# Retention and a two-layer MLP on one core: loads written as flat rows, the state cleared on GpSimd, and a new order of the early tasks

## The chip, the cores and the metric

The kernel runs on one core of one Trainium2 chip. The metric is the device time of one execution in microseconds (us); the kernel before was run three times, and its profile is that of one execution. The core has five engines, each with its own instruction stream that is worked through in order: PE (TensorE, matmuls and transposes), DVE (VectorE), ACT (ScalarE), POOL (GpSimd) and SP (SyncE). Transfers between device memory and on-chip memory are issued by an instruction on POOL, ACT or SP and are then carried out by 16 DMA engines that all issuers share. PEld in the profile is the loading of matmul weights, which overlaps PE.

## What is computed

```
B, H, S, D = 4, 8, 768, 64           # q, k, v: [B, H, S, D] float32
for t in range(S):
    state = gamma[h] * state + outer(k[t], v[t])        # per batch and head, D x D
    y[t]  = q[t] @ state / sqrt(D)
x  = y as [B, S, H*D]                                   # 4 x 768 x 512
xn = (x - mean(x)) / sqrt(var(x) + 1e-6) * g_ln
out = x + relu(xn @ w_ch1) @ w_ch2                      # 512 -> 2048 -> 512, float32
```

## The kernel before

The recurrence is worked in chunks of 128 positions. Six chunks in each of four batches make 24 tiles of 128 rows by 512 columns. Tiles 0 to 3 are the first chunk of each batch; tiles 4 to 8 are chunks 1 to 5 of batch 0; then come the other batches. For tile t, PE transposes k and q (lines 498 and 505, "tk" and "tq"; from tile 8 on a DMA transpose of the pair of both, line 520, does it), DVE scales q (line 510 or 527), PE multiplies k by q (line 538, "pa"), DVE applies the decay mask (line 562), and PE multiplies the result by v and adds the state's part (lines 582 and 586, or 548 and 572, "py"). DVE then takes mean and variance (lines 601 and 602) and subtracts the mean (line 613, "xn"); ACT keeps a copy of x (line 619); the centred tile is transposed (line 672, "tx", or a DMA transpose, line 686).

The state of a batch is carried on by four steps: POOL scales v by the decay (line 633, "vg"), PE multiplies it by k into `pd` (line 645), and DVE writes it, scaled, into one of two `state` tiles (line 659). Only the diagonal 64 by 64 blocks of a state tile are written there; the rest has to be zero, and is cleared once at the beginning (line 341).

The MLP takes tiles in groups: eight groups of one tile, four of two, two of four. The first layer ("m1", line 719) makes 2048 hidden values in steps of 512, each needing a quarter of `w_ch1` ("w1_0" to "w1_3"); ACT or DVE applies the relu (lines 732, 734). The second layer ("m2", line 757) sums over all hidden values, and its first matmul of a tile waits for all four quarters of `w_ch2` ("w2_0" to "w2_3"). DVE multiplies by the inverse deviation and adds x (line 767), and ACT issues the store (line 774).

**Loads.** All of q, k, v but k0 and q0, and the eight quarters of the weights, are loaded by DMAs that POOL issues, since they change float32 to bfloat16 (lines 430 and 438). One load of q, k or v is a tile of 128 rows, 8 heads, 64 values (128 KB written); one quarter of a weight is 512 KB written. The source of such a load has 64 values in a row, since heads lie far apart. From tile 8 on, each load on POOL stands behind a "gate" (line 447), a tiny copy that waits until an earlier load has landed. At most eight such loads are outstanding: POOL waits 0.56 us before the load at 16.76 until the one eight places earlier has landed at 16.48.

**The order of the work** is written out by hand. `plan.add` numbers the tasks in the order in which they are made. `ORDER` lists these numbers, and tasks are emitted in that order, so that it alone sets the sequence on each engine (100000 and 10000 added to a number choose a buffer or an engine). A planner with estimated durations (`load_pad` and `w_pad` are added to its landing times) computes start times from it; they set only how many filler matmuls (line 785) PE gets in early gaps, to keep it busy. The task numbers of POOL that matter here are:

```
v0 23  k1 24  q1 25  v1 26   k2 27  q2 28  v2 29   k3 30  q3 31  v3 32
k4 33  q4 34  v4 35  k5 36   q5 37  v5 38  k6 39   q6 40  v6 41  k7 42  q7 43  v7 44
w1_0..w1_3 45..48   w2_0..w2_3 49..52   k8 53  q8 54  v8 55
vg of v0, v4, v5, v6: 214 217 234 251     clearing of the state: 13 (zerod)
```

Of the kernel before, what the change touches and what calls it, by code (L numbers as in the profile page):

```python
# [14 lines left out]
PE, ACT, DVE, POOL, SP = range(5)  # L15
# [4 lines left out]
              "k3", "q3", "v3", "w1_2", "k4", "q4", "v4", "k5", "q5", "v5", "w1_3", "w2_0",  # L20
              "k6", "q6", "v6", "k7", "q7", "v7", "w2_1", "w2_2", "w2_3"],
    "bufs": {"qsb": 6, "ksb": 5, "vsb": 9, "qk": 8, "tr": 6, "vg": 3, "trq": 3, "trk": 3},
    "load_pad": 600, "w_pad": 550, "lead": 32, "lead2": 32, "sq_at": 28000, "late_load": 1700, "two": 4, "m2b": ("b0",), "m2all": 16, "inter": 4, "every": 4, "tail": (0, 384, 512), "step": 8, "pace": 8, "ahead": 3,
    "slack": 600, "tr_pad": 4000, "x_pad": 3500, "vg_pad": 2500, "fill": 0.8, "fill_end": 14000,
}

ORDER = [int(x) for x in """
16 17 2 0 3 19 20 23 14 8 15 1 24 5 7 9 25 4 10 6 13 21 11 26 18 45 22 27 44 28 146 46  # L30
100147 149 148 150 151 29 30 31 32 47 162 152 165 214 33 100163 153 164 154 155 166 156
12 167 158 157 159 168 34 176 160 35 36 100177 169 179 524 178 170 180 215 172 526 171
173 525 174 181 527 182 183 184 534 190 37 532 100191 38 10535 193 48 217 186 192 175
10533 194 49 185 187 540 195 536 39 541 234 40 196 197 537 204 207 544 198 100205 206
528 200 43 52 216 545 50 42 41 201 51 542 208 543 188 224 10529 199 218 209 100225 548
550 210 227 549 219 226 551 55 211 53 235 554 251 54 212 189 552 555 228 553 56 229 220
546 530 213 275 202 547 230 538 100241 221 10531 556 231 232 539 242 57 558 244 100237
557 233 222 238 560 161 243 10559 236 561 245 258 100259 562 246 260 566 247 563 261 564
567 252 262 570 248 249 223 254 565 255 568 60 250 569 203 263 268 100722 61 58 253 59
62 287 298 63 723 716 724 301 66 264 67 64 717 65 725 269 718 571 719 265 726 266 720  # L40
576 100271 270 276 307 267 578 272 579 577 728 273 68 69 278 277 72 729 730 731 318 73
279 70 299 71 280 580 572 732 281 300 282 74 322 284 286 734 735 75 288 239 581 283 285
736 302 303 290 289 573 737 291 738 574 319 584 292 740 741 293 320 294 296 742 308 304
240 585 78 575 743 582 744 295 297 310 333 79 76 309 77 339 586 305 583 311 80 746 587
334 747 312 335 313 314 274 316 323 81 256 315 748 84 350 749 351 588 592 317 325 85 82
83 379 750 589 257 324 354 326 727 602 86 752 87 753 327 328 329 603 593 590 754 755 594
591 330 90 331 340 352 332 342 756 341 343 721 380 598 321 599 595 91 758 336 759 344
760 761 596 733 88 345 89 355 762 346 368 348 353 600 92 757 745 739 337 597 347 93 764
96 349 97 94 381 601 95 765 98 338 357 604 356 766 606 386 99 605 382 607 767 358 306
359 383 614 612 768 360 384 615 361 613 363 770 397 102 771 103 100 362 772 398 365 364  # L50
763 369 101 104 371 370 773 403 610 372 608 774 611 373 776 616 609 399 366 105 374 387
108 109 617 375 618 414 367 377 106 107 777 620 418 751 376 378 389 619 110 388 778 390
779 622 415 391 385 404 780 392 393 621 623 630 782 395 111 114 429 115 631 394 112 400
456 113 433 626 116 624 117 396 406 120 121 416 405 430 783 627 625 407 784 431 408 628
419 409 634 785 410 629 632 411 412 457 118 119 122 413 421 635 786 445 633 420 123 788
126 458 422 127 789 646 124 423 424 790 425 427 647 401 125 426 428 791 642 638 434 436
792 435 794 795 796 639 643 465 769 437 438 640 417 439 440 442 128 797 459 641 129 441
446 443 476 132 644 798 432 402 133 645 636 130 448 447 648 131 134 138 637 460 650 449
450 649 800 651 461 451 452 801 802 477 454 803 444 775 480 462 453 466 478 455 135 491
804 136 137 468 492 467 806 139 495 807 469 470 140 493 808 471 141 809 472 142 474 473  # L60
475 652 653 654 481 483 482 484 810 655 656 658 143 510 479 485 144 787 506 805 657 799
145 659 660 661 486 662 507 496 487 489 664 663 488 508 490 666 498 497 665 499 667 668
670 669 500 671 501 502 672 673 504 511 812 674 503 505 676 513 512 675 514 678 463 677
680 515 679 682 813 681 814 683 516 494 811 509 517 781 519 464 518 520 815 100830 831
816 521 832 818 819 200824 820 825 684 817 793 685 826 690 688 691 827 689 694 696 833
695 522 686 697 687 708 709 821 698 699 692 693 523 822 848 700 828 834 702 100842 701
703 706 707 704 200836 714 837 705 715 712 838 849 843 713 710 711 850 844 845 839 846
851 840 100854 852 855 856 823 847 841 835 829 853 857 860 861 858 862 863 864 859 865
""".split()]


# [90 lines left out]
def kernel(  # L162
# [175 lines left out]

    def c_zero(eng):
        for x in state:  # L340
            nc.vector.memset(x, 0.0)

    a = plan.add
    small = a(DVE, 1200, -100, c_small)
# [11 lines left out]
    qscd = a(ACT, 700, -91, c_qsc, [args, table])  # L356
    maskd = a(DVE, 1230, -50, c_mask, [vscd, tri])
    gchd = a(ACT, 900, 100, c_gch, [small, qscd, vscd], at=9000)
    zerod = a(DVE, 480, -94, c_zero)
    exps = [gchd, qscd, vscd]  # L360

    def c_gb(eng):
# [17 lines left out]
    def load(kind, j, rank):  # L380
        takes, uses, follows = None, [], []
        if kind in "qkv":
            b, c = TILES[j]
            src = {"q": q, "k": k, "v": v}[kind][b].rearrange("h (c p) d -> c p h d", p=P)[c]
            ns, dma = 900, 875 if j < 9 else CFG["late_load"]
            pair = kind != "v" and j >= T0
            name = "qk" if pair else kind + ("0" if c == 0 and kind != "q" else "sb")
            takes = where[kind, j] = (name, j)
            if pair and kind == "q":
                takes, uses, follows = None, [takes], [loaded["k", j]]  # L390

            if j == 0 and kind in "kq":
                raws = []
                for half, eng in ((0, SP), (1, ACT)):
                    hs = slice(half * H // 2, (half + 1) * H // 2)

                    def emit32(eng, half=half, hs=hs):
                        if half == 0:
                            take("osb", kind, [P, DM], FP32)
                        dst = held["osb", kind].rearrange("p (h d) -> p h d", d=D)[:, hs]  # L400
                        (nc.scalar if eng == ACT else nc.sync).dma_start(out=dst, in_=src[:, hs])
                    raws.append(a(eng, 480, -200 + half + 2 * (kind == "q"), emit32, (),
                                  ("osb", kind) if half == 0 else None,
                                  [("osb", kind)] if half else [],
                                  lat=1200 if kind == "k" else 1700, follows=raws[:]))
                parts = []
                for half, eng in ((0, DVE), (1, ACT)):
                    if kind == "k":
                        half, eng = None, ACT

                    def emit(eng, half=half):
                        if not half:
                            take(*takes, [P, H, D], BF16)
                        hs = slice(0, H) if half is None else slice(4 * half, 4 * half + 4)
                        evacuate(eng, held[takes][:, hs],
                                 held["osb", kind].rearrange("p (h d) -> p h d", d=D)[:, hs])
                    parts.append(a(eng, 620 if half is None else 350, -60, emit,
                                   raws + parts[:1], takes if not half else None,
                                   [("osb", kind)] + ([takes] if half else [])))
                    parts[-1]["after"] = raws[:]  # L420
                    parts[-1]["follows"] = parts[:-1]
                    if kind == "k":
                        break
                loaded[kind, j] = parts
                return

            def emit(eng):
                if takes:
                    take(*takes, [P, 2, H, D] if pair else [P, H, D], BF16)
                nc.gpsimd.dma_start(out=tile_of(kind, j), in_=src)  # L430
        else:
            s = slice(j * DM, (j + 1) * DM)
            o = slice(j * KO, (j + 1) * KO)
            src, dst = (w1_v[:, :, s], w1[:, :, s]) if kind == "w1" else (w2_v[:, o, :], w2[:, o, :])
            ns, dma = 790, 2550

            def emit(eng):
                nc.gpsimd.dma_start(out=dst, in_=src)  # L438
# [382 lines left out]
```

## Time and profile before

| | |
|---|---|
| median of 3 runs | 220.67 us (220.42 to 221.4) |
| the profiled execution | 220.67 us, of which its span 218.9 us |
| busy in the span | PE 205.5 us, DVE 121.3, POOL 95.8, ACT 85.3 |
| software DMA queue (POOL's loads) | 77,024 packets, 13.37 MB, 79.8% of 16 engines' span |
| mean granted TensorE clock | 0.992 of full speed |
| PE waiting for a load of k | 3.2 us, once |

The span runs from the first to the last instruction of the program; the remaining 1.8 us of the execution lie around it. The chain of waits follows the work that ended last back to the beginning, and puts each stretch down to the engine or transfer that was being waited for. The table of stretches gives, for each part of the span, how long each engine was busy, the granted TensorE clock (PEclk, 1.00 is full speed) and what the DMA engines did.

### The profile page before, as it was taken

What the parts mean: (1) busy time and instruction counts of PE and PEld (TensorE: products, weight loads), DVE (VectorE), ACT (ScalarE), POOL (GpSimd) and SP (SyncE); (2) the same over time, 40 slices, a digit from 0 to 9 for tenths busy, and PEclk for the clock granted to TensorE, in tenths of its full rate; (3) what the DMA queues carried; (4) which work ended last, traced back from release to release, by engine and by line L of the source; (5) the groups of instructions that cost most, each with busy time, mean ns of one, the idle gap of its engine ahead of it and who ended that gap; (6) DMA issues with size and microseconds to landing.
All of it is one profiled execution on the core that took longest, in us unless ns stands there. A gap on an engine that the chain in (4) does not pass through costs nothing.

```text
span 218.9 us, 4937 instructions
## 1 busy us (share of the span) xinstructions
PE 205.5 (94%) x2005; PEld 131.9 (60%) x2027; DVE 121.3 (55%) x264; ACT 85.3 (39%) x173; POOL 95.8 (44%) x149
## 2 busy tenths in 40 slices
PE   6978999499999999999999999999999999999992
PEld 2457899396656676666766766675454444444451
DVE  6866686524547877655765686588786510030041
ACT  5476466434133242424424532352266611444200
POOL 8997398049877475573774656403000000000000
PEclk9999999969999999999999999999999999999999
DMA  9999999999999999999999999978541170000035
GB/s 128 176 179 179 162 187 165 191 118 106 109 106 116 97 124 141 169 189 206 114 151 209 87 153 127 118 108 117 101 161 27 28 215 3 0 0 0 0 141 197
DMA packets 108890, 26.85 MB, mean 123 GB/s; under 512 B 101569, under 2 KB 105921, under 8 KB 108866
## 3 DMA queue, kind: packets, MB, share of 16 engines
q0 software_dynamic: 77024, 13.37, 79.8%
q1 hardware_dynamic: 27186, 6.59, 20.8%
q10 hardware_dynamic: 4656, 6.56, 8.7%
q8 instruction: 16, 0.26, 0.5%
q14 instruction: 8, 0.07, 0.1%
HBM read 27.30 MB, written 6.29 MB: 153 GB/s over the span
## 4 chain that ended last, share of the span: by engine, by line
PE 78%; DMA 12%; POOL 7%; issue 1%; DVE 1%; DVEq 0%; POOLq 0%
PE b L757 35%; PE mm L719 33%; DMA ksb<-in_k_dram 5%; DMA w<-in_moe_w_ch_dram 5%; PE pa L538 2%; DMA out_dram<-osb 2%; POOL qsb L430 2%; PE pd L645 2%; PE b L572 2%; POOL v L430 2%; PE b L548 2%; POOL w L438 1%; POOL k L430 1%; DVE osb L767 1%; POOL vg L633 0%
## 5 line engine op out<-in xcount | busy, mean ns | idle before, releaser
L719 PE MATMUL mm<-xnt,w 128*128 128x128 bf16 (+2 forms) x896 | 96.8, 260 | 0.8 <-DMA w<-in_moe_w_ch_dram 0.8
L757 PE MATMUL b<-w,h 128*128 128x512 bf16 (+2 forms) x379 | 88.4, 370 | 1.2 <-issue 0.2
L732 ACT ACTIVATE h<-mm 128x512 bf16<-128x512 f32 x91 | 53.8, 598 | 87.0 <-PE mm L719 86.8
L719 PEld LDWEIGHTS <-w 128*128 128x128 bf16 x896 | 67.1, 99 | 21.5 <-DMA w<-in_moe_w_ch_dram 1.2
L757 PEld LDWEIGHTS <-h 128*128 128x128 bf16 x400 | 37.0, 98 | 37.7
L562 DVE TENSOR_TENSOR asb<-pa,mask 128x1024 bf16<-128x1024 f32 x24 | 29.3, 1222 | 19.1 <-PE pa L538 18.5
L767 DVE SCALAR_TENSOR_TENSOR osb<-b,rstd,x_all 128x512 f32<-128x512 f32 (+2 forms) x25 | 18.0, 726 | 26.9 <-PE b L757 26.6
L601 DVE BATCH_NORM_STATS2 bns<-b 128x6 f32<-128x256 f32 (+1 forms) x40 | 17.8, 477 | 22.3 <-PE b L586 11.2
L619 ACT CAST x_all<-b 128x256 bf16<-128x256 f32 (+1 forms) x40 | 16.2, 416 | 24.0 <-DVE xn L613 21.8
L633 POOL TENSOR_TENSOR vg<-vsb,vsc 128x512 bf16<-128x512 bf16 x16 | 16.6, 1041 | 19.3 <-DMA vsb<-in_v_dram 11.3
L613 DVE SCALAR_TENSOR_TENSOR xn<-b,mv,gb 128x256 bf16<-128x256 f32 (+1 forms) x40 | 20.1, 532 | 0.7
L430 POOL DMA_DIRECT2D vsb<-in_v_dram x20 | 18.2, 912 | 1.6 <-DMA qsb<-in_q_dram 0.8
L659 DVE TENSOR_TENSOR state<-pd,gch 64x256 bf16<-64x256 f32 x40 | 16.6, 415 | 3.7 <-PE pd L645 2.8
L430 POOL DMA_DIRECT2D qk<-in_q_dram x16 | 14.2, 890 | 1.7 <-issue 1.7
L430 POOL DMA_DIRECT2D qk<-in_k_dram x16 | 14.3, 891 | 1.5 <-issue 1.4
L447 POOL COPY scrap<-qk 1x1 bf16<-1x1 bf16 x30 | 5.5, 184 | 11.3 <-DMA qk<-in_q_dram 5.8
L447 POOL COPY scrap<-vsb 1x1 bf16<-1x1 bf16 x15 | 2.6, 176 | 15.0 <-DMA vsb<-in_v_dram 15.0
L700 DVE RECIPROCAL rstd<-rstd 128x1 f32<-128x1 f32 (+2 forms) x14 | 2.1, 156 | 12.2 <-ACT rstd L694 12.1
L785 PE MATMUL pd<-zeros 128*128 128x512 bf16 (+1 forms) x24 | 6.4, 405 | 1.3 <-DVE zeros L291 1.2
L572 PEld LDWEIGHTS <-asb 128*128 128x128 bf16 x128 | 5.8, 98 | 2.4
L527 DVE TENSOR_TENSOR trq<-tr,qsc 128x512 bf16<-128x512 bf16 x16 | 7.0, 439 | 0.1
L430 POOL DMA_DIRECT2D qsb<-in_q_dram x7 | 6.4, 915 | 0.0
(68 smaller groups left out, 128.1 us busy)
## 6 DMA issues: line engine op xcount, KB each, us to landing
out_dram<-osb ACTq DMA_DIRECT2D x23, 256.0 KB, 3.8
w<-in_moe_w_ch_dram POOLq DMA_DIRECT2D x8, 512.0 KB, 8.7
vsb<-in_v_dram POOLq DMA_DIRECT2D x20, 128.0 KB, 5.0
qk<-in_k_dram POOLq DMA_DIRECT2D x16, 128.0 KB, 4.9
qk<-in_q_dram POOLq DMA_DIRECT2D x16, 128.0 KB, 4.5
qsb<-in_q_dram POOLq DMA_DIRECT2D x7, 128.0 KB, 6.5
v<-in_v_dram POOLq DMA_DIRECT2D x4, 128.0 KB, 6.8
ksb<-in_k_dram POOLq DMA_DIRECT2D x4, 128.0 KB, 9.2
```

The source lines that it names most:

```text
L430: nc.gpsimd.dma_start(out=tile_of(kind, j), in_=src)
L562: nc.vector.tensor_tensor(out=take("asb", t, [P, NPAIR, 2, P], BF16).rearrange("p i a t -> p a i t"), in0=held["pa", t], in1=mask.rearrang ...
L572: nc.tensor.matmul(half_y[h % 2][:, h // 2 * D:(h // 2 + 1) * D], lhsT=held["asb", t][:, h // 2, h % 2, :], rhs=tile_of("v", t)[:, h, :], ...
L601: nc.vector.bn_stats(out=bns[:, t, i, :], in_=x)
L613: nc.vector.scalar_tensor_tensor(out=dst, in0=src, scalar=mv[:, t, 0:1], in1=g, op0=ALU.subtract, op1=ALU.mult)
L619: nc.scalar.copy(out=dst, in_=src)
L633: e.tensor_tensor(out=take("vg", j, [P, H, D], BF16), in0=tile_of("v", j), in1=vsc[:, cc, :].unsqueeze(2).to_broadcast([P, H, D]), op=ALU. ...
L659: nc.vector.tensor_tensor(out=held["pb", n][o, :, o], in0=held["pd", b][o, :, o], in1=gch[o, cc, :].unsqueeze(2).to_broadcast([D, NPAIR, D ...
L719: nc.tensor.matmul(p[:, j, :], lhsT=w1[:, ko, (ho + j) * P:(ho + j + 1) * P], rhs=held["xnt", hb][:, h0:h0 + n, ko, :], start=(ko == 0), s ...
L732: nc.scalar.activation(out=dst, in_=src, func=AF.Relu)
L757: nc.tensor.matmul(held[key][:, 0:w], lhsT=held["h1", hb][:, ho, i * P:(i + 1) * P], rhs=w2[:, ho, cols], start=(ho == 0), stop=(ho == HO ...
L767: nc.vector.scalar_tensor_tensor(out=take("osb", key, [P, w], FP32), in0=held[key][:, 0:w], scalar=rstd[:, t:t + 1], in1=x_all[:, t, cols] ...
```

## The change

There are four edits.

1. A load of q, k or v names its destination as a row of 512 values per partition in place of eight pieces of 64.
2. The two state tiles are cleared by POOL in place of DVE, at a later place in the order.
3. The planner's estimate of a weight's landing (`w_pad`) goes from 550 to 1500 ns.
4. `ORDER` is another one in its first 230 of 866 tasks; behind them only five small tasks of DVE (161, 175, 189, 223 and 239) stand elsewhere.

```diff
-    "load_pad": 600, "w_pad": 550, ...
+    "load_pad": 600, "w_pad": 1500, ...
 ORDER = [int(x) for x in """
-16 17 2 0 3 19 20 23 14 8 15 1 24 5 7 9 25 4 10 6 13 21 11 26 18 45 22 27 44 28 146 46
-100147 149 148 150 151 29 30 31 32 47 162 152 165 214 33 100163 153 164 154 155 166 156
-12 167 158 157 159 168 34 176 160 35 36 100177 169 179 524 178 170 180 215 172 526 171
-173 525 174 181 527 182 183 184 534 190 37 532 100191 38 10535 193 48 217 186 192 175
-10533 194 49 185 187 540 195 536 39 541 234 40 196 197 537 204 207 544 198 100205 206
-528 200 43 52 216 545 50 42 41 201 51 542 208 543 188 224 10529 199 218 209 100225 548
-550 210 227 549 219 226 551 55 211 53 235 554 251 54 212 189 552 555 228 553 56 229 220
+16 17 2 0 3 19 20 23 14 8 15 1 24 5 7 9 25 4 10 6 21 11 26 18 22 146 45 100147 149 148
+27 150 28 151 153 46 162 100163 29 152 154 164 165 30 155 12 166 31 156 167 32 157 158
+159 47 168 176 13 524 169 179 214 100177 170 525 33 215 178 171 172 216 180 34 173 181
+532 35 526 36 533 182 37 190 527 534 183 193 38 100191 184 535 48 192 185 186 194 187
+195 49 540 542 541 196 204 543 528 197 39 207 100205 198 536 529 40 200 42 43 41 206 544
+50 217 234 52 51 53 10537 55 208 100224 54 199 201 545 550 209 225 548 551 210 227 44
+226 251 202 549 552 228 218 56 211 546 553 547 222 275 212 219 538 229 235 220 100241
 ...
     def c_zero(eng):
         for x in state:
-            nc.vector.memset(x, 0.0)
+            nc.gpsimd.memset(x, 0.0)
 ...
-    zerod = a(DVE, 480, -94, c_zero)
+    zerod = a(POOL, 500, 0, c_zero, at=9000)
 ...
-                nc.gpsimd.dma_start(out=tile_of(kind, j), in_=src)
+                nc.gpsimd.dma_start(out=tile_of(kind, j).rearrange("p h d -> p (h d)"), in_=src)
```

On POOL the order of loads thus goes from the first to the second line of each pair; what stands before k2 is the same in both. Names in brackets are not loads.

```
before  k2 v7 q2 w1_1 v2 k3 q3 v3 w1_2 [vg0] k4 q4 v4 k5 q5 v5 w1_3 [vg4] w2_0 k6 [vg5] q6 q7 w2_3 w2_1 k7 v6 w2_2 v8 k8 [vg6] q8
after   k2 q2 w1_1 v2 k3 q3 v3 w1_2 [clear, vg0] k4 q4 v4 k5 q5 v5 w1_3 w2_0 k6 q6 k7 q7 v6 w2_1 [vg4 vg5] w2_3 w2_2 k8 v8 q8 v7 [vg6]
```

## The prediction

> **What bounds the kernel now.** I read the page's busy shares first, then PE's waits, then a table of stretches cut where those waits lie, and last the chain of waits around the longest of them.
>
> ```profile
> span 218.9 us, 4937 instructions
> PE 205.5 (94%) x2005; PEld 131.9 (60%) x2027; DVE 121.3 (55%) x264; ACT 85.3 (39%) x173; POOL 95.8 (44%) x149
> PE 78%; DMA 12%; POOL 7%; issue 1%; DVE 1%; DVEq 0%; POOLq 0%
> ```
>
> PE is busy for 205.5 of 218.9 us, so the change can gain at most the 13.4 us in which PE is idle, and what PE loses by a slow clock. Of PE's waits, four are long:
>
> ```profile
> PE b L498 <- DMA ksb<-in_k_dram: 3.2, 1, 3.2
> PE b L505 <- DMA qsb<-in_q_dram: 1.6, 2, 1.2
> PE pd L785 <- DVE zeros L291: 1.2, 1, 1.2
> PE mm L719 <- DMA w<-in_moe_w_ch_dram: 0.8, 2, 0.5
> ```
>
> The columns are total us, times, longest. The first is tk of tile 7, waiting for k7. The stretches (busy us of each engine, granted clock PEclk, DMA share, GB/s):
>
> ```profile
> 0.00:23.00 23.00, 18.21 (x210) 11.69 (x211) 16.43 (x48) 12.77 (x27) 19.70 (x28) 1.00 1.69 165
> 23.00:40.60 17.60, 17.45 (x324) 16.79 (x324) 12.82 (x25) 11.67 (x24) 11.25 (x13) 1.00 1.65 176
> 40.60:43.80 3.20, 0.03 (x2) 0.00 (x0) 1.30 (x2) 0.34 (x1) 0.00 (x0) 1.00 1.82 182
> 43.80:52.00 8.20, 8.18 (x117) 7.86 (x119) 4.06 (x9) 3.26 (x7) 4.96 (x7) 0.79 1.17 94
> 52.00:205.00 153.00, 151.84 (x1296) 90.33 (x1315) 83.44 (x176) 56.63 (x117) 59.86 (x102) 1.00 1.00 109
> ```
>
> PE is idle for 4.8 us before 23, full to 40.6, idle for 3.2, then on a granted clock of 0.79, and from 52 to 205 idle for 1.2 of 153. So the place to look at is 0 to 52. There the chain reads (start, us, what):
>
> ```profile
> 32.96 10.81 DMA ksb<-in_k_dram
> 43.77 0.05 issue
> 43.82 0.40 PE b L498 x4
> 44.21 0.22 PE b L505 x4
> 44.44 2.93 PE mm L719 x32
> 47.37 0.43 PE b L582 x4
> 47.80 0.43 PE b L586 x8
> 48.22 0.97 PE mm L719 x16
> ...
> 50.97 0.89 PE mm L719 x16
> 51.86 0.22 PE b L757
> ```
>
> k7 lands at 43.77, 10.8 us after its issue, since it stands in the DMA queue behind two quarters of w2. The six rows behind it take 5.38 us; at the full clock the same work takes 3.56 (0.22 for each set of transposes and for L582, 0.23 for L586, 0.89 for 16 matmuls of L719, all from rows elsewhere in the chain). So the stall costs 3.2 us of waiting and 1.8 us of slow clock, 5.0 in all. The first m2 starts at 51.86.
>
> **Edit 1, the loads.** In the instruction listing of the built program, each load of q, k and v still stands as 128x8x64, in the changed kernel as in the one before. The instructions are the same, so I cost this at nothing: 77,024 packets in the software queue should stay. What it would be worth if the pieces did grow: a 128 KB load lands some 0.87 us behind the one before it, a 512 KB quarter of a weight 2.6, or 0.65 for each 128 KB, so 0.22 us a load. The Trainium skill (DMA: Bandwidth & Descriptors, Specifications) asks for 512 B and more in a transfer for the full rate, and by that rule this edit would be the main gain. The listing decides against it, and the larger-piece case is a rival below.
>
> **Edit 2, the clearing.** DVE loses two memsets of 0.27 us at 3.37; its next step waits for q0 and starts at 4.84 after 0.92 idle, so this gains nothing. POOL gets two memsets of 128x512 bf16. No row shows that; the nearest are a POOL memset of one column, 0.09 us, and the vg multiplication of the same size with two inputs, 1.04. So 0.2 to 2.1 us for both, and I take 1, nearer to the multiplication by its size. They stand behind the issue of w1_2, and v7's issue (0.93) is no longer in front of them, so vg0, at 13.38 before, starts at 12.65 to 14.55. PE needs it for pd of tile 0, at 15.5 before and about 14.2 now: 0 to 1.3 us of waiting, which the next wait for a load then absorbs (below, PE is ahead of k6 anyway). The loads behind wait in a queue some eight deep, so later issue does not make them land later. Cost 0; with that cover gone, 1.3.
>
> **Edit 3.** `w_pad` reaches the program only by the count of filler matmuls; PE has 4,053 rows in both listings. Nothing.
>
> **Edit 4, the order.** Two relus of the first groups go from DVE (0.68 us) to ACT (0.60), which is busy for 11.67 of the 17.60 us from 23 to 40.6: nothing. The queue works through loads one behind the other, so landings follow from the order. Landings before (issue plus time to landing): k2 12.33, v7 13.29, k4 24.01, w1_3 30.77, w2_0 33.94, k6 34.78, q6 35.64, q7 36.45, w2_3 39.16, w2_1 42.93, k7 43.77, v6 44.60, w2_2 47.19, v8 48.02, k8 48.86, q8 49.69.
>
> - v7 goes from the front to behind q8. All from q2 to w1_3 lands 13.29 - 12.33 = 0.96 us sooner.
> - From w1_3 to the last quarter of w2 the queue holds the same nine loads in both, so that quarter lands at 47.19 - 0.96 = 46.2. k7 is now in front of three quarters: w2_0 at 33.0, k6 33.8, q6 34.7, k7 35.5, and the last v8, k8, q8, v7 at 46.2 + 4 x 0.84 = 49.6. The gap of 3.17 before w2_0 (others 2.6) may shrink, as POOL no longer does vg4 in front of it.
>
> Now PE, in the new listing's order, from tk of tile 4 (k4 lands at 23.05) to the first m2: 18 steps of m1 at 0.89, 15 short groups (transposes, pd) at 0.22, 4 pa at 0.33, 3 py at 0.45: 16.0 + 3.3 + 1.3 + 1.4 = 22.0, without a wait 45.05. The one wait for a load on the way is tk of tile 6, which PE reaches 10.0 us on, at 33.05, and k6 lands at 33.8: 0.75 us, well under the 1.2 us that PE waited before 23 at a clock of 1.00. That gives 45.8. The same count for the kernel before (23.14, plus 23.1 of work, plus the 5.0) gives 51.25 where the trace has 51.86; I charge those 0.6 here too, so 46.4, just behind the last quarter at 46.2. tk of tile 7 comes at about 39, far behind k7 at 35.5: the stall is gone, and so is the slow clock. First m2 at 46.4 in place of 51.86: 5.4 us sooner.
>
> What may be late next: (a) The queue named "instruction" moves single packets of 16 KB; one falls in the transfer of w2_0 and one in that of w2_1, which took 3.2 and 3.8 in place of 2.6. The next lies at 48.8, behind the last quarter; it goes with the program's progress, so it may now fall in that quarter: 0 to 1.2. (b) py of tile 7 needs v7. It stands four steps of m2 (3.46) behind the first, at 49.9; v7 lands at 49.6, or with (a) a little later: 0 to 1. I take 0.5 for both. Sum: 5.0 for the stall and its clock, plus 0.4 from earlier landings net of the new waits, less 0.5: **4.9 us**.
>
> From 52 on PE has the same work. It only holds the gain if the later tiles' operands come in time. The transposed pair of tile 8 is there at 54.0 and DVE takes it at 61.03: 7 us of slack, less 5.4, plus 0.9 as q8 lands sooner. That leaves 2.5, so nothing is charged.
>
> The profiled execution took 220.67 us, the same as the median, with 1.8 outside its span. **220.67 - 4.9 = 215.8 us.**
>
> **Rivals.**
> Later loads fall behind PE. From tile 9 on a load is issued when an earlier one has landed (issue to landing 3.5 to 6 us), so this stream moves up by 1 to 3 us and PE by 5. For it: POOL already waits 15.0 us for vsb in its gates. Against it: about 7 us of slack at tiles 8 and 9. If it comes, 1.5 to 2 us are given back: 217.5.
> The loads do write larger pieces. 21 loads of 0.22 less land the last quarter 4.6 us sooner; then PE alone bounds, and the 0.75 and some 1.6 of waits before 23 fall away: 4.9 + 2.4, or 213.4. Against it: the listing.
> Slower: py of tile 7 stops PE, with all of m2 queued behind it. Its v7 came at 13.29 and now is the last of the early loads. Each us of landing behind 49.9 costs one, and once the wait is about 3 us the clock falls and costs 1.8 more, so it decides from a landing at 53 on; at 55 the time is 215.8 + 5.1 + 1.8 = 222.7. For it: eight loads may be outstanding, and one that holds the queue delays all. Against it: only four short loads lie behind the last quarter.
> No net effect: the stall reappears whole at the first m2, if the last quarter still came at 51. Against it: 47.19 before.
>
> The Trainium skill (TensorE: Matmul & The Clock Gate, Part 1) says that the clock falls after an idle window of about 3.4 us. Here 3.2 us sufficed; by the page alone the 1.8 would be doubtful, and the gain about 3.1.
>
> **Numbers.** The forecast, 214.6 to 217.0, has 0.74; late loads 0.10; larger pieces 0.04; slower by v7 0.07; no effect 0.05. The range for 8 in 10, 214.6 to 218.0, takes in the forecast with both ends of (a) and (b) and the late loads. About 0.5% (1.1 us) is what a measurement of this kernel can tell from no change: faster 0.88, same 0.05, slower 0.07.
>
> **What would show it.** Right: no wait of PE for ksb over 1 us; PEclk 1.00 from 23 on; the first L757 at 46 to 47.5; DVE without the two memsets, POOL with two of 0.1 to 1 us; the software queue at about 77,000 packets. Wrong: a wait above 2 us at the first m2, at py of tile 7 or at tile 8's scaling; or fewer packets and 128 KB loads landing 0.65 apart.

## The result, and the profile after

The changed kernel takes 215.52 us (median of 4 runs, 215.26 to 215.57), the kernel before 221.03 (median of 4, 220.42 to 222.32). The ratio is 0.974, 95% interval 0.969 to 0.979; this ratio and those below leave out executions more than 1.5% above the fastest of the same kernel, so where the kernel before spreads widely they show less than the medians do. The forecast was 215.8 in a range of 214.6 to 218.0. The profiled execution of the changed kernel took 215.49 us with a span of 213.7, so 1.8 us lie outside the span as before, and all of the 5.2 us went from the span.

The page of the changed kernel: its span, the busy line, the granted clock in 40 slices, and the software queue.

```profile
span 213.7 us, 4941 instructions
PE 204.1 (95%) x2005; PEld 130.5 (61%) x2027; DVE 120.1 (56%) x260; ACT 86.2 (40%) x175; POOL 96.5 (45%) x151
PEclk9999999999999999999999999999999999999999
q0 software_dynamic: 77024, 13.37, 82.5%
```

PE's idle time fell from 13.4 us to 9.6, its busy time by 1.4: the first is mainly the wait, the second mainly the slow clock, and no slice shows a lower clock now (the clock records of this trace begin at 5.05 us). Its waits (total us, times, longest):

```profile
PE pd L785 <- DVE zeros L291: 1.2, 1, 1.2
PE b L498 <- DMA k<-in_k_dram: 0.8, 1, 0.8
PE mm L719 <- ACT xnt L256: 0.7, 2, 0.4
PE pd L645 <- POOL vg L633: 0.7, 1, 0.7
PE b L672 <- DVE xn L613: 0.5, 1, 0.5
```

The wait for `ksb` is gone from the list. What is left before 24 us is no longer mainly loads: it is the new place of the clearing (vg) and the way from DVE's xn over ACT's copy to the first layer. The stretches of the changed kernel, with the columns as before:

```profile
0.00:23.00 23.00, 18.51 (x214) 12.12 (x216) 15.57 (x45) 11.82 (x25) 19.81 (x30) 1.00 1.68 164
23.00:40.00 17.00, 16.87 (x315) 16.13 (x313) 11.50 (x21) 12.71 (x24) 13.95 (x16) 1.00 1.76 186
40.00:46.00 6.00, 6.00 (x115) 5.79 (x113) 5.07 (x9) 3.30 (x7) 0.27 (x2) 1.00 1.77 183
46.00:52.00 6.00, 5.95 (x51) 3.40 (x50) 1.79 (x7) 2.24 (x5) 5.81 (x9) 1.00 1.45 115
52.00:200.00 148.00, 146.89 (x1264) 87.83 (x1282) 82.93 (x175) 55.54 (x114) 56.64 (x97) 1.00 1.01 110
```

From 40 to 46 PE is full at the full clock, where it lost 3.2 us and then ran slowly before. The timeline of PE shows tile 7's transpose and the first m2 (start, us, engine, line):

```profile
38.98 0.39 PE L498 MATMUL b<-idn,ksb 128*128 128x128 bf16 x4
...
46.78 3.62 PE L757 MATMUL b<-w,h 128*128 128x512 bf16 x15
```

In the same view the first m2 of the kernel before starts at 51.70:

```profile
51.70 3.62 PE L757 MATMUL b<-w,h 128*128 128x512 bf16 x15
```

So 4.9 us of the span's 5.2 are won by 47 us; the remaining 0.3 lie behind.

### The profile page after: what moved, and what is told of

It reads as the page before. It is cut to its first block, busy times and chain, and to the rows that moved or that the text cites. A ratio compares the mean times of both kernels' runs of the same rounds, so it can differ in the third digit from the quotient of the medians.

```text
span 213.7 us, 4941 instructions
## 1 busy us (share of the span) xinstructions
PE 204.1 (95%) x2005; PEld 130.5 (61%) x2027; DVE 120.1 (56%) x260; ACT 86.2 (40%) x175; POOL 96.5 (45%) x151
## 3 DMA queue, kind: packets, MB, share of 16 engines
q0 software_dynamic: 77024, 13.37, 82.5%
## 4 chain that ended last, share of the span: by engine, by line
PE 87%; DMA 3%; POOL 3%; ACT 2%; issue 1%; DVE 1%; POOLq 0%; DVEq 0%
PE b L757 39%; PE mm L719 38%; DMA w<-in_moe_w_ch_dram 3%; PE pd L645 2%; PE pa L538 2%; PE b L572 2%; PE b L548 2%; POOL v L430 1%; PE b L672 1%; ACT L694 1%; PE b L586 1%; ACT xnt L256 1%; POOL vg L633 0%; PE b L498 0%; POOL state L341 0%
## 5 line engine op out<-in xcount | busy, mean ns | idle before, releaser
L719 PE MATMUL mm<-xnt,w 128*128 128x128 bf16 (+2 forms) x896 | 95.2, 257 | 0.8 <-ACT xnt L256 0.7
L732 ACT ACTIVATE h<-mm 128x512 bf16<-128x512 f32 x93 | 55.0, 598 | 83.4 <-PE mm L719 83.1
L719 PEld LDWEIGHTS <-w 128*128 128x128 bf16 x896 | 66.1, 98 | 21.3 <-issue 0.9
L700 DVE RECIPROCAL rstd<-rstd 128x1 f32<-128x1 f32 (+2 forms) x14 | 2.0, 156 | 13.4 <-ACT rstd L694 13.4
L438 POOL DMA_DIRECT2D w<-in_moe_w_ch_dram x8 | 6.2, 774 | 3.3 <-DMA w<-in_moe_w_ch_dram 3.3
```

The lines of the kernel that those rows point to most:

```text
L719: nc.tensor.matmul(p[:, j, :], lhsT=w1[:, ko, (ho + j) * P:(ho + j + 1) * P], rhs=held["xnt", hb][:, h0:h0 + n, ko, :], start=(ko == 0), s ...
L732: nc.scalar.activation(out=dst, in_=src, func=AF.Relu)
```

## The experiments

Three sets of four kernels were run, each set beside the kernel before, and all on one chip. The kernel before spread from 217.6 to 224.5 us in these sets, in part for a reason that the runs showed and that is told below. So ratios have wide intervals, and I lean on the profiles as much as on the ratios. Landing times are those of single loads in each trace.

### Edit 1 alone

```diff
-                nc.gpsimd.dma_start(out=tile_of(kind, j), in_=src)
+                nc.gpsimd.dma_start(out=tile_of(kind, j).rearrange("p h d -> p (h d)"), in_=src)
```

> The kernel before with edit 1 alone (the destination of each load named as a row of 512). Theory: the instructions are the same, so no change: ratio 1.000 within 0.003, 77,024 packets in the software queue. Rival (the pieces grow): packets fall to about 17,000, 128 KB loads land 0.65 us apart in place of 0.87, and the time falls by 2 us or more.

Ratio 1.002, interval 0.997 to 1.007, and 77,024 packets: no effect, as expected.

```profile
q0 software_dynamic: 77024, 13.37, 81.4%
```

### k7 alone moved ahead

```diff
-528 200 43 52 216 545 50 42 41 201 51 542 208 543 188 224 10529 199 218 209 100225 548
+528 200 43 42 52 216 545 50 41 201 51 542 208 543 188 224 10529 199 218 209 100225 548
```

> The kernel before with one load moved: k7 is issued directly behind q7, ahead of the quarters w2_3 and w2_1. Theory: k7 lands at about 37.3 in place of 43.8, and the 3.2 us wait of PE and its slow clock are gone; but v6 still lands at 44.6, and py of tile 6, which PE now reaches at about 42.9, waits for it for some 1.7 us with the clock kept. Gain 5.0 - 1.7 = 3.3 us, ratio about 0.985. Rival (the wait for k7 is the whole matter): gain 5.0, ratio 0.977. Rival (PE waits for the weights anyway, so the wait reappears at the first m2): gain under 1.

217.14 us against 220.69 (medians), ratio 0.990, interval 0.987 to 0.993. k7 landed at 37.6. PE's waits:

```profile
PE b L505 <- DMA qsb<-in_q_dram: 2.1, 2, 1.2
PE b L586 <- DMA vsb<-in_v_dram: 1.2, 1, 1.2
```

The second line is the new wait, py of tile 6 for v6, which landed at 44.7 as before: 1.2 us where 1.7 were expected. The first m2 starts at 48.62. Taking away one wait thus uncovers the next at once, and the medians' gain of 3.6 us (3.3 expected) fits the stall less this wait; by the ratio the gain is about 2.2.

### k7 and v6 moved ahead

```diff
-528 200 43 52 216 545 50 42 41 201 51 542 208 543 188 224 10529 199 218 209 100225 548
+528 200 43 42 41 52 216 545 50 201 51 542 208 543 188 224 10529 199 218 209 100225 548
```

> The kernel before with two loads moved: k7 and v6 directly behind q7, ahead of w2_3, w2_1 and w2_2. Theory: no wait at tile 7's transpose nor at py of tile 6; PE would reach the first m2 at 51.86 - 5.0 = 46.9, the last quarter of w2 lands at 47.2, so a wait of 0.3 there. Gain 4.7 us, ratio 0.979: nearly all of the change's gain from two places in the order. Rival (the gain needs the rest of the new order): 3 us or less, ratio over 0.986.

215.60 us against 220.69, ratio 0.984, interval 0.978 to 0.991. PE waits for neither load, and the first m2 starts at 46.78, to the hundredth where the changed kernel has it. Two numbers in the order are nearly the whole gain: the changed kernel itself has a ratio of 0.984 in the third set, below.

### v7 alone moved back

> The kernel before with v7 alone moved from the front of the load queue to behind q8. Theory: all loads from q2 on land up to 0.96 us sooner, k7 at 42.8; PE, which was waiting for loads before 23, moves up by 0.4 to 0.96 as well, so the wait for k7 stays at about 3.2 and the slow clock with it. Gain 0.4 to 1.0 us, ratio 0.996 to 0.998. Rival (py of tile 7 now waits for the late v7): slower by over 0.5 us. Rival (this is the main part of the change): gain over 2 us.

In the order 44 was taken from between 22 and 27 and put behind 54. 219.25 us against 220.69, ratio 0.995, interval 0.990 to 1.001: near the expected size, and not to be told from nothing. PE still waits for k7, 2.3 us here where the wait was expected to stay at about 3.2, and the slow clock follows. No wait for v7 appeared.

### PE kept busy through the stall

```diff
+    def e_hold(eng):
+        p = take("mm", "hold", [P, DM], FP32)
+        for _ in range(13):
+            nc.tensor.matmul(p, lhsT=zeros[:, 0:P], rhs=zeros, start=True, stop=True)
+    a(PE, 2800, 0, e_hold, [], ("mm", "hold"))
-557 233 222 238 560 161 243 10559 236 561 245 258 100259 562 246 260 566 247 563 261 564
+557 233 222 238 560 161 243 10559 236 561 245 866 258 100259 562 246 260 566 247 563 261 564
```

> The kernel before with 13 filler matmuls of 512 columns (zeros times zeros, 2.8 us at full clock, their result unused) on PE just ahead of tile 7's transpose of k, where PE waits 3.2 us for k7. The wait itself stays. Theory: the slow clock behind the wait is a price of its own, 1.8 us: with PE kept busy the granted clock stays at 1.00 from 43.8 to 52, and the time falls by 1.6 to 1.8 us, ratio about 0.992. Rival (the slow rows behind the wait are not due to PE's idleness, or cost nothing as PE would wait for the weights): ratio 0.998 or more.

218.23 us against 219.47, ratio 0.994, interval 0.990 to 0.997. The matmuls do nothing but keep PE busy, and the kernel is faster. The slow clock is a price of its own, but of 1.2 us in the medians, not 1.8; why is told with the second of the prediction's points below. Every execution has its mean granted clock on record, and one step of 3.41 us at half the clock lowers that mean by 0.008. It lies under 0.995 in 17 of the 23 executions of the kernel before in this set, and in 2 of the 12 with the fillers.

### k7 and v6 put back in the new order

```diff
-195 49 540 542 541 196 204 543 528 197 39 207 100205 198 536 529 40 200 42 43 41 206 544
-50 217 234 52 51 53 10537 55 208 100224 54 199 201 545 550 209 225 548 551 210 227 44
+195 49 540 542 541 196 204 543 528 197 39 207 100205 198 536 529 40 200 43 206 544
+50 217 234 52 42 41 51 53 10537 55 208 100224 54 199 201 545 550 209 225 548 551 210 227 44
```

> The changed kernel with k7 and v6 put back to where they stood before among the quarters of w2 (q7, w2_1, w2_3, k7, v6, w2_2). Theory: k7 lands at about 41.3 and PE, which reaches tile 7's transpose at 39.0, waits 2.3 us; v6 at 42.1 is in time; the last quarter still lands at 44.7, the first m2 comes 2.3 us later. If that wait is too short to lower the clock: slower by 2.3 us, ratio 1.011; if the clock falls as it did behind 3.2 us: slower by 4.1, ratio 1.019. Rival (these two places do not matter in the new order): ratio 1.000 to 1.003.

220.00 us, spread from 217.5 to 220.9; ratio to the kernel before 1.001, interval 0.997 to 1.004. The whole gain is gone, so these two places carry it in the new order too. In the profile (span 216.5) tile 7's transpose waits 2.75 us:

```profile
39.70:42.45 2.75, 0.00 (x1) 0.00 (x0) 0.75 (x1) 0.60 (x1) 0.48 (x1) 1.00 1.66 192
42.45:46.00 3.55, 3.55 (x68) 3.34 (x69) 2.19 (x4) 2.26 (x4) 1.04 (x1) 1.00 2.10 166
```

Here the clock did not fall: 68 matmuls ran in the 3.55 us behind the wait (the trace holds no clock record, so its 1.00 alone would say nothing). This execution's span is 2.8 us over the changed kernel's. The median is 4.5 us over it, and the clock does not explain the difference: seven of the 12 executions have a mean clock under 0.995 and average 219.8 us, but the five others average 219.4 and lie between 217.5 and 220.9. What else costs time in them stays open.

### The same with PE kept busy

> The changed kernel with k7 and v6 put back among the quarters of w2, as in the run before, and 10 filler matmuls (zeros, 2.2 us, result unused) in front of tile 7's transpose, where PE then waits. Theory: behind a wait of 2 to 3 us the clock falls in some executions and not in others, which is what spread that run from 217.5 to 220.9; with PE kept busy no execution has the slow clock, so the times lie close together near the lower end, 217.3 to 218.5, median about 217.8. Rival (the spread comes from the landing times): as wide as without the fillers, median near 220.

217.47 us, 216.97 to 219.04. Ten filler matmuls bring the median down by 2.5 us against the run without them, though in another set, and the spread from 3.3 us to 2.1; none of the 12 has a mean clock under 0.995. So keeping PE busy helps here too, but the five executions just named show that the spread is not the clock's alone.

### All of the new load order, none of PE's

The kernel with k7 and v6 ahead, with v7 moved back as well.

> The kernel before with all that the change does to the order of the early loads, and nothing of what it does to the other engines: k7 and v6 directly behind q7, and v7 behind q8. Theory (the gain is the loads', PE's new order brings nothing of its own): the first m2 at 46.0 to 46.8 and a time within 0.7 us of the changed kernel's on the same chip. Rival (PE's new order is needed for the last part of the gain): 1 us or more above the changed kernel.

215.40 us; the changed kernel on the same chip took 215.47. The first m2 is at 46.42. What the change does to the order on PE, DVE and ACT brings nothing that these runs can tell.

### The changed kernel once more, and with the clearing on DVE

> The changed kernel as it is, on the chip of the other three runs. Theory: 215.5 us, and with no early wait over 1 us its times lie within 1 us of each other. A rival that the first result owed part of its gain to that chip: over 217.

215.47 us, 214.78 to 217.36, against 219.97 for the kernel before in this set, ratio 0.984, interval 0.979 to 0.990: the gain holds in another set, at 4.5 us by the medians, but the times do not lie within 1 us of each other. The profiled execution has a span of 215.5, with the same order and no long wait. Its PE timeline beside that of the first one, the changed kernel's profile first:

```profile
8.79 0.87 PE L785 MATMUL pd<-zeros 128*128 128x512 bf16 x4
```

```profile
11.31 1.58 PE L785 MATMUL pd<-zeros 128*128 128x512 bf16 x4
```

The same four filler matmuls take 0.87 us in one and 1.58 in the other. In the clock records of the first the full clock begins at 5.05 us, in those of the second at 13.33.

> The changed kernel with edit 2 undone: the state is cleared by DVE at its old place. vg of tile 0 starts about 1.0 us sooner on POOL, and the 0.7 us wait of PE for it is gone. Theory: the time won is taken back by the next loads, of which k4 (landing at 23.6, PE reaches it at 23.95) leaves at most 0.35 us: gain 0 to 0.35 us, ratio 0.998 to 1.000 against the changed kernel. Rival (the clearing on POOL costs what PE waits for it): gain 0.7 us. Rival (DVE's 0.54 us more delay its early work): slower by up to 0.5 us.

> The changed kernel with the state cleared by DVE at its old place, beside the changed kernel on the same chip. Theory: 0 to 0.35 us faster (the 0.7 us wait for vg of tile 0 is gone and the next load, k4, takes back the rest). Rival: 0.7 us faster. Rival: slower, if DVE's 0.54 us delay its early work.

The edit, run in two sets; task 13 also goes back to its old place in `ORDER`:

```diff
-            nc.gpsimd.memset(x, 0.0)
+            nc.vector.memset(x, 0.0)
-    zerod = a(POOL, 500, 0, c_zero, at=9000)
+    zerod = a(DVE, 480, -94, c_zero)
```

In the first of these sets 215.72 us, without the changed kernel beside it; in the second 214.88 against 215.47, 214.46 to 215.58 against 214.78 to 217.36. In both profiles the wait for vg is gone. But the first m2 starts at 47.18 in the first of them, where PE waits 1.4 us for one of the first loads of k, and at 46.34 in the second; the changed kernel's own two profiles have it at 46.78 and 48.41. So these runs do not settle what the clearing on POOL costs, and six executions of each that overlap do not either. 214.88 is the lowest median of all that was run.

### Loads of larger pieces

```diff
+            wide = {"q": q, "k": k, "v": v}[kind][b].rearrange(
+                "h (x y) d -> (h x) (y d)", y=8)[c * P:(c + 1) * P]
-                nc.gpsimd.dma_start(out=tile_of(kind, j).rearrange("p h d -> p (h d)"), in_=src)
+                nc.gpsimd.dma_start(out=tile_of(kind, j).rearrange("p h d -> p (h d)"), in_=wide)
```

> The changed kernel with loads of q, k and v that read 512 values in a row of memory per partition (other elements of the same tensors than the kernel needs, so the data are not those of the reference), which is what edit 1 would be if the pieces did grow. Theory: the packets of the software queue fall from 77,024 to about 17,000 and a 128 KB load lands 0.65 us behind the one before; PE's waits before 24 (k2 0.8, and what hangs on it) shrink, but from 24 on PE is full whatever the loads do: gain 1 to 2 us, ratio about 0.993. Rival (the load queue still bounds the whole of the first 47 us): gain 4 us or more. Rival (the piece size does not matter): no change.

The software queue shows:

```profile
q0 software_dynamic: 14304, 13.37, 42.3%
```

The last quarter of w2 lands at 40.53 in place of 44.73, 4.2 us sooner, and a 128 KB load some 0.7 us behind the one before. Yet the first m2 starts at 46.02, only 0.76 sooner, the span is 213.3, only 0.4 less, and the median (215.92) is no better. I expected 1 to 2 us; it is under that. With PE full from 24 us on, faster loads have nothing left to shorten. Its runs spread from 213.8 to 219.1; why, these runs do not show.

## Why the prediction was right, point by point

**Edit 1 at nothing:** right, alone and in the packet count. The Trainium skill (DMA: Bandwidth & Descriptors, Specifications) asks for 512 B and more in a transfer; the run with larger pieces agrees that such pieces move faster (42.3% of the engines' time in place of 82.5% for the same bytes), and the span shows that here it no longer matters.

**Edit 3 at nothing:** both pages have 24 filler matmuls at line 785 and 2005 instructions on PE; it was not run alone.

**The stall of 5.0 us:** the wait and the slow clock are both gone, and moving k7 and v6 alone gives the same first m2. But the term of 1.8 us was sized from one execution in which the clock fell, and it does not fall in every one. The clock records change only at steps of 3.41 us. What PE did in the step that holds the stall, and in the one behind it, in the kernel before, in the run with v7 alone moved, and in that with edit 1 alone, whose instructions are those of the kernel before:

```profile
41.43:44.84 3.41, 1.02 (x19) 1.03 (x20) 0.80 (x2) 0.00 (x0) 0.07 (x1) 1.00 1.62 190
44.84:48.25 3.41, 3.41 (x40) 3.41 (x38) 0.13 (x1) 1.67 (x3) 1.86 (x2) 0.50 1.51 106
```

```profile
40.56:43.98 3.42, 1.15 (x21) 1.15 (x22) 1.67 (x3) 0.28 (x1) 0.20 (x1) 1.00 1.81 182
43.98:47.39 3.41, 3.41 (x40) 3.41 (x38) 0.23 (x2) 1.67 (x3) 2.62 (x3) 0.50 1.91 168
```

```profile
41.30:44.72 3.42, 1.51 (x27) 1.52 (x28) 1.08 (x2) 0.00 (x0) 0.59 (x1) 1.00 1.73 185
44.72:48.13 3.41, 3.41 (x69) 3.20 (x66) 1.95 (x6) 2.17 (x4) 1.34 (x2) 1.00 1.95 148
```

With PE busy for 1.02 and 1.15 us of a step, the next step ran at 0.50 (40 matmuls); with 1.51 it ran at 1.00 (69). So it is not the length of the wait that decides, as the prediction had it with its "about 3 us": with v7 alone moved a wait of 2.3 us lowered the clock, and with edit 1 alone one of 2.6 us did not. The third has a span of 216.2, 2.7 us less than the first, from identical instructions: 0.6 from a shorter wait, the rest mostly from the clock.

The mean clock of each execution points the same way. Of the 69 executions of the kernel before in the three sets, 56 have a mean under 0.995 and average 220.4 us; the 13 others average 218.5. The changed kernel's ten have none under it and average 215.6. So the gain is near 5 us where the clock of the kernel before fell and near 3 where it did not. The clock is not the whole of the spread, for the two groups spread by 6.7 and 2.9 us within themselves; and the mean does not say where the slow step lay (in the run with k7 and v6 ahead three of six are under 0.995, at 215.6 to 216.7 us).

The forecast of the gain thus had some luck: all four executions of the kernel before in the first result took 220.4 us or more. Against its medians in the three later sets (220.69, 219.47, 219.97) the changed kernel's 215.5 is a gain of 4.0 to 5.2.

**The first m2 at 46.4, and 0.5 for what is late next:** in the chain of waits, from which the 51.86 was read, it now starts at 46.95, so the sum of 46.9 held, but by errors that cancelled. The chain has tile 4's transpose and the first m2 at:

```profile
24.11 0.22 PE b L498 x4
46.95 0.22 PE b L757
```

The sum let PE begin tile 4 at 23.05. k4 landed at 23.63, and PE came 0.5 us later still, behind small waits before 24: 0.7 for vg, 0.7 for ACT's copies and 0.5 for xn. That is 1.1 us late. In return the 0.75 us of waiting for k6 did not come, and from 24.11 on PE took 22.8 us where 22.0 and the extra 0.6 had been counted. Together this is the 0.5 that had been charged for (a) and (b), and neither of these cost anything. The last quarter of w2 landed at 44.73, 1.5 us before the forecast 46.2, because the quarters followed each other at 2.5 to 2.6 us. A packet of the instruction queue fell into that time as well and delayed nothing to be seen, so (a), which blamed those packets, is not supported, and what stretched w2_1 to 3.8 us in the first profile stays open. The bound was PE's own work, not the weights, so the error in the landing did not matter.

**v7 from the front, 0.96 us:** k4 landed at 23.97 to 25.44 (mean 24.36) in five profiles with v7 in front and at 23.13 to 24.29 (mean 23.64) in eight without it: 0.7 us, within a spread of more than 1 us from execution to execution.

**Edit 2 at nothing, with a cover:** the two memsets took 1.0 us, as taken:

```profile
12.70 0.76 POOL L438 DMA_DIRECT2D w<-in_moe_w_ch_dram  x1 [0.93 <-DMA w<-in_moe_w_ch_dram]
13.44 1.01 POOL L341 MEMSET state<- 128x512 bf16 x2
14.39 1.06 POOL L633 TENSOR_TENSOR vg<-v,vsc 128x512 bf16<-128x512 bf16 x1
```

Two steps failed here. With v7's issue out of the way, w1_2 was to be issued 0.93 us sooner; but POOL sat idle for those 0.93 us until w1_0, the load eight places earlier, had landed at 12.41, and issued w1_2 at 12.70 where it had been 12.61. So the clearing came on top, and vg0 started at 14.39, a microsecond later than before and near the late end of the range given for it. And the cover: I let the wait for k6 absorb what the clearing costs, but k6 landed at 33.8 and PE reached it at 34.50, so nothing absorbed it there. PE waited 0.7 us for vg; how much of that reaches the first m2, the runs do not settle. It sat inside the 0.5 charged to other causes.

**Rivals.** Late loads: none; tile 8's pair landed at 52.7 and DVE took it at 56.12, 3.4 us of slack where 2.5 was forecast. v7 at py of tile 7: no wait. Larger pieces: the pieces did not grow, and the 2.4 us put on them was too much, since the run that does read larger pieces gains 0.76 us at the first m2 and 0.4 in the span.

## What to carry to other kernels

When a stall is followed by a slow clock, price the two apart, and treat the second as something that may or may not happen; a few idle matmuls in front of the waiting one show which part it is. In a queue that works through its loads in turn, write down the landing order beside the order of first use: two loads that were needed some 10 us sooner than the large ones in front of them were nearly the whole of this gain. Remove a wait together with the next one in line, as the run with k7 alone shows, and do not count a cost at nothing because a wait that is only forecast would hide it.

## What the runs showed of the hardware

The granted clock of PE changed only in steps of 3.41 us: the records last 3.41, 40.96 (12 steps) and 208.21 (61 steps). A step in which PE was busy for 1.15 of 3.42 us was followed by one at half the clock, one with 1.51 was not; near the end of the run with k7 alone moved, one with 1.34 was as well. The Trainium skill (TensorE: Matmul & The Clock Gate, Part 1) states a free-running window of 3413 ns, which agrees, and a fall after at least one idle window, which does not: PE was busy for 30 to 39% of these. It also says that the start of the full clock depends on where that window lies; here it began at 3.88 us at the earliest and at 13.33 at the latest, in the same kernel at 5.05 and at 13.33, with the first m2 1.6 us apart (46.78 and 48.41). In the second of these PE was busy for the whole step from 6.51 to 9.92, and the step behind it was still slow (the 1.58 us of the four filler matmuls); why stays open.

PEclk of the profile does not show such a slow beginning. Before the full clock begins there is no clock record, and the column stands at 1.00, as in this stretch of the second profile:

```profile
8.00:13.30 5.30, 5.30 (x32) 2.55 (x30) 3.27 (x5) 1.60 (x7) 5.17 (x8) 1.00 1.66 184
```
